# ScalarE's high part of the last unit moves behind its copy of the first product, VectorE's low part one place later

## The chip, the cores and the metric

The kernel runs on one core of a Trainium2 chip. The metric is device time in microseconds (us) of the whole kernel, lower is better. A core has a matrix engine (TensorE; in the profile PE for its matmuls and PEld for its weight loads), three engines for elementwise work (VectorE or DVE, ScalarE or ACT, GpSimd or POOL) and SyncE (SP), which here only issues DMAs. Every engine works through its own queue in program order; between engines there are only semaphores.

## What is computed

Three layers in a row: masked attention, a mixture of eight experts with two chosen per token, and a gated layer on 2304 tokens. Only the gated layer is touched:

```python
rms = np.sqrt(np.mean(x * x, axis=-1, keepdims=True) + 1e-06)
xn = x / rms * rms_g
g = xn @ w_gate
silu = g * (1.0 / (1.0 + np.exp(-g)))
val = xn @ w_val
return (silu * val @ w_out).astype(np.float32)
```

Here x is 2304 x 512, w_gate and w_val are 512 x 1536, w_out is 1536 x 512.

## The kernel before

**Precision.** A number is kept as a high part (rounded to the matmul's format) and a low part (what the rounding left). `mm3` (L149 to L151) makes one product of three matmuls: high by high, high by low, low by high. So wherever a matmul operand is prepared, ScalarE writes the high part and VectorE then subtracts it from the full value to get the low part.

**Tiling.** The gated layer makes three passes of 768 tokens (two groups of 384) over 12 blocks of 128 columns of w_gate and w_val. Four blocks of pass 0 are done plainly; the other 32 (eight of pass 0, twelve each of passes 1 and 2) are *units*. A unit takes both token groups, both halves of the 512 inputs, and gate and value together, as a 2 x 2 by 2 x 2 block product with seven products instead of eight. `product` makes one of them (six matmuls of 384 columns), in the order P1, P6, P7, P5, P4, P2, P3, and `nextb` gives it one of only two PSUM banks, 3 and 6, in turn. A bank comes free when its product has been read: P1 by ScalarE's copy into `p1` (L1294), the others by VectorE's additions. The results are `sgb` (gate times value of the second token group, L1328) and `sga` (of the first, L1338, after P3 at the end of the unit).

**The result's way on.** `to_h` has ScalarE copy the high part of `sga` or `sgb` into a tile `ha` (L1125) and returns the low part's subtraction on VectorE (L1127) for later. `om` multiplies `ha` by w_out: three matmuls of 512 columns. The next unit runs the three `om` of `sgb` after P1, P6 and P7, and the three of `sga` after P5, P4 and P2.

**What else is in a unit.** `whi` and `wlo` split the weights of the next two units in four pieces (L1195 on ScalarE; L1208 on VectorE in pass 0; from pass 1 on the low parts come back by DMA). `comb` runs one of four steps that combine the experts' outputs for the next pass: `weigh` is ScalarE's scaling (L856), then come VectorE's addition (L859) with ScalarE's squares (L860), a root (L863, L864), and a scaling (L874). `tile_T`, in the units with blocks 4 to 9 of passes 0 and 1, transposes a tile of these on TensorE after P1 (L1237), into the *next* of the same two banks, and ScalarE copies it to `xT` (L1239). `extra` splits operands of the next pass, in some units with a copy on ScalarE (L1164) and a subtraction on VectorE (L1166).

**Banks with a transpose.** Without one, P1 takes bank A, P6 bank B, P7 bank A. With one, P1 takes A, the transposes B, P6 A again, P7 B. There P6 needs the copy of P1 (L1294), and P7 the copy to `xT` (L1239). Twelve units are like this.

The order of all queues is written out by hand in `unit`; no scheduler changes it. Around the change it was, at a unit's end and the next one's start: product P3, VectorE's addition and multiplication into `sga`, ScalarE's high part of `sga`, ScalarE's `whi(n + 2, 0)`; then product P1, the copy to `p1`, `comb`, the low part of `sga`, `wlo(n + 1, 0)`, `whi(n + 1, 1)`.

Of the kernel before, what the change touches and what calls it, by code (L numbers as in the profile page):

```python
# [24 lines left out]
def attn_moe_swiglu(ctx: ExitStack, tc: tile.TileContext, q, k, v, w_gate, w_noise, noise, w1, w2,  # L25
# [816 lines left out]
    def fetch(t):  # L842
        YG[t] = []
        for kk in range(2):
            y = buf("yg")
            nc.gpsimd.indirect_dma_start(y, None, yd, bass.IndirectOffsetOnAxis(  # L846
                ap=posu[:, kk, t:t + 1], axis=0))
            YG[t].append(y)

    def combine_parts(t):  # L850
        ya, y2 = YG.pop(t)
        ms = bc.tile([128, 2], F32, name="ms", bufs=2)
        X2[t] = (ya, ms)

        def weigh():
            nc.scalar.activation(ya, ya, AF.Copy, scale=wts[:, t, 0:1])  # L856

        def add():
            nc.vector.scalar_tensor_tensor(ya, y2, wts[:, t, 1:2], ya, op0=OP.mult, op1=OP.add)  # L859
            nc.scalar.activation(y2, ya, AF.Square, accum_out=ms[:, 0:1])  # L860

        def root():
            nc.vector.tensor_scalar(ms[:, 1:2], ms[:, 0:1], 1.0 / DM, 1e-6, op0=OP.mult, op1=OP.add)  # L863
            nc.gpsimd.tensor_tensor(ms[:, 0:1], ms[:, 1:2], mhalf, op=OP.pow)  # L864

        return [weigh, add, root, lambda: norm(t)]
# [246 lines left out]
    sga, sgb, u2, u3, p1 = (gx.tile([128, 384], F32, name=n) for n in ("sga", "sgb", "u2", "u3", "p1"))  # L1113
# [4 lines left out]
    def nextb():  # L1118
        turn["g"] += 1
        return bank[(3, 6)[turn["g"] % 2]][:, :384]  # L1120

    def to_h(p, f, i, sg):

        h = keep.tile([128, 2, 384], F32R, name="ha", bufs=2)
        nc.scalar.copy(h[:, 0], sg)  # L1125
        HG[p, f, i] = h
        return lambda: V.tensor_tensor(h[:, 1], sg, h[:, 0].bitcast(F32), op=OP.subtract)  # L1127

    def om(p, f, i, t):

        h = HG[p, f, i]
        w = slot(cuse["O", f // 2])
        o = (f % 2) * 512
        b = ob[3 * i + t]
        mm3(b, h, w, (slice(t * 128, (t + 1) * 128),), (slice(o, o + 512),), f == 0, f == NFC - 1)
        if f == NFC - 1:
            y = buf("o")
            if t % 2 == 0 or p + 1 < NP:
                nc.scalar.copy(y, b)  # L1139
            else:  # L1140
                V.tensor_copy(y, b)
            r = (p * 6 + i * 3 + t) * 128
            nc.sync.dma_start(out[r:r + 128, :], y)
# [35 lines left out]
    def wload(n):  # L1179
        if n < len(cols):  # L1180
            f = cols[n][1]
            b, c = (wb1, wc1) if n % 2 else [keep.tile([128, 1024], F32, name="stage", bufs=2) for _ in range(2)]
            a = ud[UD.index(("G", f))]
            nc.sync.dma_start(b[:, :512], a[:, :512])
            nc.sync.dma_start(b[:, 512:768], a[:, 768:])
            nc.sync.dma_start(c, uc[f])
            WS[n] = b, c
# [3 lines left out]
    def whi(n, i):  # L1191
        if n < len(cols):
            d = BW[n % 2].rearrange("p s k n -> p s (k n)")
            b, c = WS[n]
            nc.scalar.copy(d[:, 0, slice(*PIECE[i])], (c[:, :512], b[:, :512], c[:, 512:], b[:, 512:768])[i])  # L1195

    def wlo(n, i):

        if n < len(cols):
            p, f = cols[n]  # L1200
            d = BW[n % 2].rearrange("p s k n -> p s (k n)")
            b, c = WS[n]
            sl = slice(*PIECE[i])
            if (p and (p - 1, f) in cols):
                if i == 0:
                    nc.sync.dma_start(d[:, 1].bitcast(F32), ul[f])
            else:
                V.tensor_tensor(d[:, 1, sl], (c[:, :512], b[:, :512], c[:, 512:], b[:, 512:768])[i],  # L1208
                                d[:, 0, sl].bitcast(F32), op=OP.subtract)
                if i == 3:  # L1210
                    nc.sync.dma_start(ul[f], d[:, 1].bitcast(F32))
# [14 lines left out]
    def prod(n, name, b):  # L1226
        a, k = PROD[name]
        for c in range(2):
            o = b, BW[n % 2], SOP[cols[n][0], a], (k, slice(c * 128, (c + 1) * 128)), (c,)
            mm3(*o, c == 0, c == 1)  # L1230

    def tile_T(t):
        ya, _ = X2.pop(t)
        turn["g"] += 1
        b = bank[(3, 6)[turn["g"] % 2]]
        for c in range(4):
            nc.tensor.transpose(b[:, c * 128:(c + 1) * 128], ya[:, c * 128:(c + 1) * 128], identf)  # L1237
        o = (t % 3) * 128
        nc.scalar.copy(xT[t // 3 % 2][:, :, o:o + 128], b.rearrange("p (c n) -> p c n", c=4))  # L1239


    def extras(p, f):
        if p + 1 == NP:
            return []

        def halves(n):
            return [(lambda h=h: split_op(p + 1, n, h, 0), lambda h=h: split_op(p + 1, n, h, 1)) for h in range(2)]

        def part(n, k):
            return None, lambda: sums(n, slice(k * 128, k * 128 + 128))  # L1250

        a11, s2, s3, s1, a22, a12, s4 = (halves(n) for n in ORDER)
        s4s = [(None, lambda k=k: sums("S4", slice(k * 192, k * 192 + 192))) for k in range(2)]
        return {7: [*a11, part("S1", 0), part("S2", 0), part("S3", 0)],
                8: [part(n, 1) for n in ("S1", "S2", "S3")],
                9: [part(n, 2) for n in ("S1", "S2", "S3")] + s2,
                10: s3 + s4s, 11: s1 + a22 + [a12[0]], 12: [a12[1]] + s4}.get(f, [])

    def unit(n):
        p, f = cols[n]  # L1260
        pp_, pf = (p, f - 1) if f else (p - 1, NFC - 1)
        t6 = 6 * (p + 1)
        more = p + 1 < NP
        ex = deque(extras(p, f) if f else extras(p - 1, NFC) if p else [])
        todo = []
        cmb = combine_parts(t6 + f - 3) if more and 3 <= f < 9 else []
        wload(n + 2)

        def om_(i, t):
            if (pp_, pf, i) in HG:  # L1270
                om(pp_, pf, i, t)

        def extra(k=1, last=False):

            while todo:
                todo.pop(0)()
            for _ in range(0 if last else k):
                if ex:
                    hi, lo = ex.popleft()
                    if hi is not None:  # L1280
                        hi()
                    todo.append(lo)

        def comb():
            if cmb:
                cmb.pop(0)()

        def product(name):
            b = nextb()
            prod(n, name, b)  # L1290
            return b

        b = product("P1")
        nc.scalar.copy(p1, b)  # L1294
        comb()
        LO.pop(0)()
        wlo(n + 1, 0)
        whi(n + 1, 1)
        extra()
        om_(1, 0)  # L1300
        if more and 4 <= f < 10:
            tile_T(t6 + f - 4)
        b = product("P6")
        V.tensor_add(u2, b, p1)
        wlo(n + 1, 1)
        whi(n + 1, 2)
        comb()
        extra()
        om_(1, 1)
        b = product("P7")  # L1310
        V.tensor_add(u3, b, u2)
        wlo(n + 1, 2)
        whi(n + 1, 3)
        comb()
        extra()
        om_(1, 2)
        b = product("P5")
        V.tensor_add(sgb, b, u3)
        V.tensor_add(u2, b, u2)
        comb()  # L1320
        extra(2)
        om_(0, 0)
        b = product("P4")
        V.tensor_add(u3, b, u3)  # L1324
        nc.scalar.activation(u3, u3, AF.Silu)  # L1325
        wlo(n + 1, 3)
        extra(last=True)
        V.tensor_mul(sgb, sgb, u3)  # L1328
        lo = to_h(p, f, 1, sgb)
        om_(0, 1)  # L1330
        b = product("P2")
        V.tensor_add(sga, b, p1)
        nc.scalar.activation(sga, sga, AF.Silu)
        lo()
        om_(0, 2)
        b = product("P3")
        V.tensor_add(u2, b, u2)  # L1337
        V.tensor_mul(sga, sga, u2)  # L1338
        LO.append(to_h(p, f, 0, sga))
        whi(n + 2, 0)  # L1340
        if more and 2 <= f < 8:
            fetch(t6 + f - 2)
# [66 lines left out]
            split_op(0, "S4", h, k)  # L1409
    for t in range(3):  # L1410
        om(0, 2, 1, t)
    LO = [lambda: None]
    HG = {k: h for k, h in HG.items() if k == (0, NREG - 1, 1)}
    for n in range(len(cols)):
        unit(n)
    LO.pop()()
    for i in (1, 0):
        for t in range(3):
# [31 lines left out]
```

## Time and profile before

| | |
|---|---|
| time, median of 3 runs | 1095.3 us (1095.11 to 1097.02) |
| the profiled execution, its own time | 1100.19 us |
| its span, first to last instruction | 1098.4 us |
| TensorE matmuls busy | 1051.4 us, 96% |
| TensorE weight loads busy | 944.9 us, 86% |
| VectorE busy | 700.1 us, 64% |
| ScalarE busy | 494.5 us, 45% |

The profile is one execution. Busy times are sums over the whole span; the units begin at about 704 us of it and end at about 1090 us. A row of the timeline has a start, a duration, the engine, the line and the operation, and in brackets how long the engine had stood idle and who released it. Starts of consecutive rows can be nearer than the durations, since instructions overlap in the pipeline, so what an instruction costs its engine is read from start to start.

### The profile page before, as it was taken

What the parts mean: (1) busy time and instruction counts of PE and PEld (TensorE: products, weight loads), DVE (VectorE), ACT (ScalarE), POOL (GpSimd) and SP (SyncE); (2) the same over time, 40 slices, a digit from 0 to 9 for tenths busy, and PEclk for the clock granted to TensorE, in tenths of its full rate; (3) what the DMA queues carried; (4) which work ended last, traced back from release to release, by engine and by line L of the source; (5) the groups of instructions that cost most, each with busy time, mean ns of one, the idle gap of its engine ahead of it and who ended that gap; (6) DMA issues with size and microseconds to landing.
All of it is one profiled execution on the core that took longest, in us unless ns stands there. A gap on an engine that the chain in (4) does not pass through costs nothing. (4 is left out here: it accounts for less than half of the span.)

```text
span 1098.4 us, 17694 instructions
## 1 busy us (share of the span) xinstructions
PE 1051.4 (96%) x6309; PEld 944.9 (86%) x6309; DVE 700.1 (64%) x1489; ACT 494.5 (45%) x1044; POOL 223.1 (20%) x261
## 2 busy tenths in 40 slices
PE   7988989999999999999999999999999999999998
PEld 5776777889989999999898989888999888999997
DVE  4666665457788788876354144878876566754554
ACT  4766652353443444443344144545454554543342
POOL 6565210303232323222200034111000220000000
PEclk8989889999999999999999999999999999999999
DMA  9977522358798898775444133455456554464431
GB/s 162 206 177 162 129 62 64 96 176 267 267 300 279 284 287 296 261 246 184 164 155 143 48 115 98 146 203 174 168 201 231 195 175 148 159 216 166 140 135 58
DMA packets 179418, 196.13 MB, mean 179 GB/s; under 512 B 66816, under 2 KB 135424, under 8 KB 179328
## 3 DMA queue, kind: packets, MB, share of 16 engines
q1 hardware_dynamic: 169264, 172.37, 49.8%
q0 software_dynamic: 9920, 22.35, 7.7%
q8 instruction: 50, 0.82, 0.3%
q14 instruction: 40, 0.33, 0.1%
q10 hardware_dynamic: 144, 0.26, 0.1%
HBM read 140.88 MB, written 54.00 MB: 177 GB/s over the span
## 5 line engine op out<-in xcount | busy, mean ns | idle before, releaser
L149 PE MATMUL bank<-xta,low 128*128 128x384 f32 x376 | 128.0, 340 | 3.1 <-DVE posu L956 2.0
L151 PE MATMUL bank<-xta,low 128*128 128x384 f32 x376 | 127.9, 340 | 0.0
L150 PE MATMUL bank<-xta,low 128*128 128x384 f32 x376 | 127.7, 340 | 0.0
L149 PE MATMUL bank<-ring,ha 128*128 128x512 f32 x288 | 114.3, 397 | 0.0
L150 PE MATMUL bank<-ring,ha 128*128 128x512 f32 x288 | 114.0, 396 | 0.0
L151 PE MATMUL bank<-ring,ha 128*128 128x512 f32 x288 | 114.0, 396 | 0.0
L149 PE MATMUL bank<-low 128*128 128x384 f32 x264 | 89.8, 340 | 7.3 <-ACT p L1294 7.2
L150 PE MATMUL bank<-low 128*128 128x384 f32 x264 | 89.7, 340 | 0.0
L151 PE MATMUL bank<-low 128*128 128x384 f32 x264 | 89.5, 339 | 0.0
L1030 POOL TENSOR_TENSOR dm<-dm,da 128x512 f32<-128x512 f32 x36 | 46.7, 1296 | 203.7 <-DVE da L1028 101.8
L162 ACT ACTIVATE ha<-bank 128x384 fp32r<-128x384 f32 x64 | 31.4, 490 | 116.5 <-PE bank L151 116.4
L149 PEld LDWEIGHTS bank<-xta,low 128*128 128x128 f32 x376 | 71.3, 190 | 11.4 <-issue 3.3
L163 DVE SCALAR_TENSOR_TENSOR ha<-bank,ha 128x384 fp32r<-128x384 f32 x64 | 35.4, 553 | 63.4 <-ACT ha L162 63.3
L150 PEld LDWEIGHTS bank<-xta,low 128*128 128x128 f32 x376 | 71.2, 189 | 4.9
L151 PEld LDWEIGHTS bank<-xta,low 128*128 128x128 f32 x376 | 71.2, 189 | 0.0
L846 POOL DMA_INDIRECT buf<-yd,posu x36 | 38.5, 1069 | 155.2 <-DMA yd<-buf 98.6
L1325 ACT ACTIVATE u<-u 128x384 f32<-128x384 f32 x32 | 16.8, 526 | 115.7 <-DVE u L1324 115.7
L151 PEld LDWEIGHTS bank<-ring,ha 128*128 128x128 f32 x288 | 54.0, 187 | 12.4 <-DVE ha L1127 0.3
L149 PEld LDWEIGHTS bank<-low 128*128 128x128 f32 x264 | 49.6, 188 | 15.7 <-ACT p L1294 9.8
L132 DVE TENSOR_TENSOR low<-stage,low 128x1024 fp32r<-128x1024 f32 x34 | 42.6, 1256 | 23.2 <-ACT low L131 21.4
L830 POOL DMA_INDIRECT buf<-xd,mapu x37 | 47.8, 1291 | 46.7 <-DVE posu L956 16.6
L149 PEld LDWEIGHTS bank<-ring,ha 128*128 128x128 f32 x288 | 54.1, 188 | 3.1 <-ACT ha L1125 0.3
(284 smaller groups left out, 2780.9 us busy)
## 6 DMA issues: line engine op xcount, KB each, us to landing
stage<-in_moe_w_dram SPq DMA_DIRECT2D x128, 256.0 KB
low<-ul SPq DMA_DIRECT2D x20, 896.0 KB
ul<-low SPq DMA_DIRECT2D x12, 896.0 KB
yd<-buf SPq DMA_DIRECT2D x40, 256.0 KB
ud<-dm SPq DMA_DIRECT2D x36, 256.0 KB
stage<-uc SPq DMA_DIRECT2D x16, 512.0 KB
wc<-uc SPq DMA_DIRECT2D x16, 512.0 KB
yd<-zero SPq DMA_DIRECT2D x28, 256.0 KB
```

The lines of the kernel that those rows point to most:

```text
L132: lo_engine.tensor_tensor(r[:, 1], st, r[:, 0].bitcast(F32), op=OP.subtract)
L149: nc.tensor.matmul(o, l[(slice(None), 0) + lsl], r[(slice(None), 0) + rsl], start=first, stop=False)
L150: nc.tensor.matmul(o, l[(slice(None), 0) + lsl], r[(slice(None), 1) + rsl], start=False, stop=False)
L151: nc.tensor.matmul(o, l[(slice(None), 1) + lsl], r[(slice(None), 0) + rsl], start=False, stop=last)
L162: nc.scalar.activation(h[:, 0], p, AF.Relu)
L163: nc.vector.scalar_tensor_tensor(h[:, 1], p, 0.0, h[:, 0].bitcast(F32), op0=OP.max, op1=OP.subtract)
L830: nc.gpsimd.indirect_dma_start(t, None, xd, bass.IndirectOffsetOnAxis(ap=mapu[:, e * NT + j:e * NT + j + 1], axis=0))
L846: nc.gpsimd.indirect_dma_start(y, None, yd, bass.IndirectOffsetOnAxis(ap=posu[:, kk, t:t + 1], axis=0))
L1030: nc.gpsimd.tensor_tensor(m, m, a.bitcast(F32), op=OP.add)
L1325: nc.scalar.activation(u3, u3, AF.Silu)
```

## The change

The high part of `sga` is no longer queued at the end of its own unit. It is kept in a list and queued in the next unit right behind the copy of P1; the low part's subtraction, which was queued before `wlo(n + 1, 0)`, now stands behind VectorE's addition that reads P6. For the first unit and behind the last one the lists are set up so that each part is queued once.

```diff
         b = product("P1")
         nc.scalar.copy(p1, b)
+        HI.pop(0)()
         comb()
-        LO.pop(0)()
         wlo(n + 1, 0)
         whi(n + 1, 1)
         extra()
...
         b = product("P6")
         V.tensor_add(u2, b, p1)
+        for lo in LO[:1]:
+            LO.remove(lo)
+            lo()
         wlo(n + 1, 1)
...
         V.tensor_mul(sga, sga, u2)
-        LO.append(to_h(p, f, 0, sga))
+        HI.append(lambda: LO.append(to_h(p, f, 0, sga)))
         whi(n + 2, 0)
...
-    LO = [lambda: None]
+    HI, LO = [lambda: None], []
...
     for n in range(len(cols)):
         unit(n)
+    HI.pop()()
     LO.pop()()
```

ScalarE's queue, where the second unit of pass 0 (block 5) ends and the third (block 6) begins, before: `sga` is turned into `ha` first, then comes the weight piece (`wc_5918` to `low`), then P1's bank into `p_6865`.

```order
L1333 ACTIVATE sga<-sga 128x384
L1125 CAST ha<-sga 128x384
L1195 CAST low<-wc_5918 128x512
L1294 COPY p_6865<-bank_104 128x384
L856 ACTIVATE buf<-buf,wts 128x512
L1195 CAST low<-wb_6866 128x512
L1239 COPY xT_5916<-bank_107 128x4x128
```

The same place in the changed kernel, whose line numbers from the second product on are 3 higher:

```order
L1336 ACTIVATE sga<-sga 128x384
L1195 CAST low<-wc_5918 128x512
L1294 COPY p_6865<-bank_104 128x384
L1125 CAST ha<-sga 128x384
L856 ACTIVATE buf<-buf,wts 128x512
L1195 CAST low<-wb_6866 128x512
L1239 COPY xT_5916<-bank_107 128x4x128
```

The cast of `sga` went two rows down, past the weight piece and the copy of P1; all the others kept their order.

VectorE's queue at the same place, before: the multiplication into `sga`, its low part, a weight piece, then the addition that reads P6's bank and `p`.

```order
L1338 TENSOR_TENSOR sga<-sga,u_6863 128x384
L1127 TENSOR_TENSOR ha<-sga,ha 128x384
L1208 TENSOR_TENSOR low<-wc_5918,low 128x512
L1304 TENSOR_TENSOR u_6863<-bank_104,p_6865 128x384
L1208 TENSOR_TENSOR low<-wb_6866,low 128x512
L859 SCALAR_TENSOR_TENSOR buf<-buf,wts 128x512
L1311 TENSOR_TENSOR u_6864<-bank_107,u_6863 128x384
```

In the changed kernel:

```order
L1341 TENSOR_TENSOR sga<-sga,u_6863 128x384
L1208 TENSOR_TENSOR low<-wc_5918,low 128x512
L1304 TENSOR_TENSOR u_6863<-bank_104,p_6865 128x384
L1127 TENSOR_TENSOR ha<-sga,ha 128x384
L1208 TENSOR_TENSOR low<-wb_6866,low 128x512
L859 SCALAR_TENSOR_TENSOR buf<-buf,wts 128x512
L1314 TENSOR_TENSOR u_6864<-bank_107,u_6863 128x384
```

The low part went past a weight piece and the addition of P6. On TensorE, SyncE and GpSimd no instruction changed its place.

## Rows read from the trace of the kernel before

**Rows 1.** The page: its head, and TensorE's busy time, share and instructions.

```profile
span 1098.4 us, 17694 instructions
...
PE 1051.4 (96%) x6309; PEld 944.9 (86%) x6309; DVE 700.1 (64%) x1489; ACT 494.5 (45%) x1044; POOL 223.1 (20%) x261
```

**Rows 2.** Busy time by stretch: PE, PEld, DVE, ACT, POOL; granted clock; DMA share; GB/s.

```profile
840.00:930.00 90.00, 86.14 (x448) 78.39 (x448) 54.98 (x109) 42.98 (x93) 15.29 (x16) 1.00 0.55 184
930.00:1090.00 160.00, 160.00 (x829) 148.66 (x828) 89.15 (x164) 64.03 (x135) 0.00 (x0) 1.00 0.43 145
```

**Rows 3.** Waits from 690 us on: total us, times, longest us.

```profile
PEld bank L149 <- ACT p L1294: 9.8, 11, 1.1
PE bank L149 <- ACT p L1294: 7.2, 11, 0.8
...
PEld bank L149 <- ACT xT L1239: 0.9, 2, 0.5
```

**Rows 4.** Timeline of TensorE, third unit of pass 0: P1's end to P6's beginning.

```profile
728.21 0.33 PE L151 MATMUL bank<-xta,low 128*128 128x384 f32 x1
...
729.08 0.60 PE L1237 MATMUL bank<-identf,buf 128*128 128x128 f32 x4
730.31 0.45 PE L149 MATMUL bank<-low 128*128 128x384 f32 x1 [0.64 <-ACT p L1294]
730.60 0.34 PE L150 MATMUL bank<-low 128*128 128x384 f32 x1
...
730.31 0.19 PEld L149 LDWEIGHTS bank<-low 128*128 128x128 f32 x1 [0.87 <-ACT p L1294]
```

**Rows 5.** Timeline of TensorE, first unit: transposes, P6's second matmul, P7's first.

```profile
705.06 0.60 PE L1237 MATMUL bank<-identf,buf 128*128 128x128 f32 x4
...
705.67 0.34 PE L150 MATMUL bank<-low 128*128 128x384 f32 x1
...
707.24 0.33 PE L149 MATMUL bank<-low 128*128 128x384 f32 x1
```

**Rows 6.** Timeline of ScalarE, third unit of pass 0.

```profile
728.85 0.51 ACT L1125 CAST ha<-sga 128x384 fp32r<-128x384 f32 x1 [1.95 <-DVE sga L1338]
729.27 0.61 ACT L1195 CAST low<-wc 128x512 fp32r<-128x512 f32 x1
729.79 0.47 ACT L1294 COPY p<-bank 128x384 f32<-128x384 f32 x1
730.16 0.72 ACT L856 ACTIVATE buf<-buf,wts 128x512 f32<-128x512 f32 x1
...
731.29 0.59 ACT L1239 COPY xT<-bank 128x512 f32<-128x512 f32 x1
```

**Rows 7.** How soon ScalarE follows TensorE: last matmul and copy, pass 1.

```profile
809.36 0.40 PE L151 MATMUL bank<-ring,ha 128*128 128x512 f32 x1
...
809.79 0.59 ACT L1139 COPY buf<-bank 128x512 f32<-128x512 f32 x1 [0.25 <-PE bank L151]
```

**Rows 8.** Timeline of SyncE: the load that the cast at 729.27 reads.

```profile
714.97 1.12 SPq L1186 DMA_DIRECT2D wc<-uc  x1
```

**Rows 9.** Timeline of ScalarE, unit with block 7 of pass 0.

```profile
744.24 0.51 ACT L1164 CAST low<-xT 128x384 fp32r<-128x384 f32 x1
```

**Rows 10.** Timeline of VectorE: third unit of pass 0, then block 7.

```profile
729.40 0.56 DVE L1127 TENSOR_TENSOR ha<-sga,ha 128x384 fp32r<-128x384 f32 x1 [0.64 <-ACT ha L1125]
729.92 0.69 DVE L1208 TENSOR_TENSOR low<-wc,low 128x512 fp32r<-128x512 f32 x1
731.76 0.56 DVE L1304 TENSOR_TENSOR u<-bank,p 128x384 f32<-128x384 f32 x1 [1.15 <-PE bank L151]
...
733.50 0.56 DVE L1311 TENSOR_TENSOR u<-bank,u 128x384 f32<-128x384 f32 x1
...
735.21 0.56 DVE L1318 TENSOR_TENSOR sgb<-bank,u 128x384 f32<-128x384 f32 x1 [0.48 <-PE bank L151]
...
748.48 0.55 DVE L1318 TENSOR_TENSOR sgb<-bank,u 128x384 f32<-128x384 f32 x1
```

## The prediction

> **What bounds the kernel now.** I read the page first: TensorE's matmuls are busy for 96% of a span of 1098.4 us [rows 1], so time can only come out of the places where TensorE stands still. The busy time by stretch says where these are: from 930 us on it is busy in all 160.00 of 160 us, while in the 90 us from 840, where the units carry transposes, it lacks 3.9 us [rows 2]. The granted clock is 1.00 in both stretches, the 2.4 GHz level, so no stretch has a slower clock to win back. The list of waits then names the cause: from 690 us on TensorE waits for ScalarE's copy of P1 (L1294) 11 times, 7.2 us in its matmuls and 9.8 us in its weight loads [rows 3]. The timeline of one such unit shows the pattern. P1's last matmul runs from 728.21 to 728.54, the transposes start at 729.08, and then P6, which needs P1's bank back, stands until 730.31 [rows 4]. ScalarE explains the lateness: the copy starts only at 729.79, 1.25 us after P1 was ready, because the high part of `sga` (728.85, released by VectorE's multiplication) and a weight piece (729.27) stand ahead of it [rows 6]. The eleven are the units with a transpose but the first one; the first has no last unit's high part ahead of its copy and does not wait. In the other twenty units P6 has another bank, and the copy's lateness is covered by P6 itself.
>
> **What a removed stall is worth.** The idle time of 0.64 us in P6's row understates it, since the first matmul after it is also longer (0.45 us) [rows 4]. I compare with the first unit, where nothing waits: from the start of the transposes to P6's second matmul it takes 705.67 - 705.06 = 0.61 us [rows 5], in the stalled unit 730.60 - 729.08 = 1.52 us [rows 4]. The stall costs 0.91 us. Ten are alike, and one is the longest of the list, 1.1 us [rows 3]: 10 x 0.91 + 1.1 = 10.2 us in all. This is the most that the change can give back, since the trace shows in these units only two further waits, on `xT` [rows 3], beside short ones in the first unit that nothing of the change touches.
> The Trainium skill, "Perfetto Trace Analysis", section Identifying the Most-Contended Engine, says that matmul busy time misleads because pipelined matmuls look smaller, and that weight-load time is the better measure. By its measure the sum would be 9.8 us and by matmul idle time 7.2 us; the trace, with 0.91 us from start to start, sides with the weight loads.
>
> **The high part moved (ScalarE).** Nothing is added or removed, one cast of 0.42 us from start to start (728.85 to 729.27) moves behind the copy [rows 6]. What does the copy wait for then? The weight piece still ahead of it needs its load, which was issued at 714.97 [rows 8], 13.6 us before P1 ends; and it can run while ScalarE stood idle 1.95 us before the high part [rows 6]. So I take it as done, and the copy starts with P1's end. ScalarE follows TensorE by 809.79 - (809.36 + 0.40) = 0.03 us [rows 7], which gives 728.57, and an end at 729.04. P6 on the unstalled course would start its second matmul at 729.08 + 0.61 = 729.69; the copy is out of the way by over half a microsecond, and the stall should go as a whole.
>
> **What is late next: the copy to `xT`.** P7 needs its bank. In the new order ScalarE's row of starts is copy 728.57, high part 0.37 later (728.94; its multiplication was done by 728.85), `weigh` 0.42 later (729.36), then `weigh` and a weight piece 731.29 - 730.16 = 1.13 us (730.49), and 0.59 us for the copy itself: 731.08 [rows 6]. A release takes about 0.05 us (copy end 729.79 + 0.47 = 730.26, P6 at 730.31 [rows 4, 6]), so P7 could start at 731.13. Unstalled it starts 707.24 - 705.06 = 2.18 us after the transposes [rows 5], here at 731.26. So 0.13 us is left, of which a late release would take 0.1 for the longer first matmul: nearly nothing, and this is the tightest place. I take zero loss; the bound on the other side is the 0.42 us of the moved cast.
> Three kinds of unit differ. In the two with block 7 a further cast of the same size as the moved one (0.51 us at 744.24 [rows 9], so 0.42 us from start to start) stands ahead of the copy to `xT`; these are the two waits of 0.9 us in all [rows 3]. There the copy to `xT` comes earlier by the 1.22 us that the copy of P1 gains (729.79 to 728.57) less 0.42 us, so 0.8 us, while P6 comes 0.91 us earlier: the wait grows by 0.1 us, 0.2 us for both. In the first stalled unit TensorE's P1 is nearer to the multiplication and the high part may hold the queue: 0.1 us. In the two with block 9 there is no `weigh`, and the margin is wide.
>
> **The low part moved (VectorE).** It no longer waits 0.64 us for ScalarE ahead of a weight piece, but costs about 0.5 us (729.40 to 729.92) behind P6's addition [rows 10]. The addition of P7 behind it starts later after its product by that much; in this unit VectorE had 0.48 us of idle time ahead of P5's addition (735.21), and that takes it up [rows 10]. P7's bank is wanted again by P4, behind P5, so a P7 addition that is 0.5 us later still ends before P5's addition and nobody waits: cost 0. Without that cover it would be 0.5 us a unit. The low part itself and the high part are read by `om` only behind P5, two products later. The units without a transpose and the end of the kernel keep their time: TensorE is busy without a gap there, and the last high part has the same neighbours as before.
>
> **Sum.** 10.2 - 0.2 - 0.1 = 9.9 us; I take 9.8, as seven units have only that margin of 0.03 us behind a late release. The profiled execution is at 1100.19 us with a span of 1098.4 us, 0.3 to 0.4% above the median of 1095.3; scaled, 9.8 us stays 9.8. **Forecast 1085.5 us**, its own range 1084.4 to 1086.8: all of 10.2 us and a quicker run below, 0.2 us more lost in each of seven units above.
>
> **Rivals.**
> *Weight loads hidden in the wait.* If P6's first weights were loaded while the copy runs, only the idle time of the matmuls is lost now, and 7.2 us come back: 1088.1 us. Against it: P6's weight load starts at 730.31, with its matmul and not ahead of it [rows 4]. Chance 0.07. The Trainium skill's "TensorE: Matmul & The Clock Gate", section Architectural detail, says that TensorE may pull weight loads ahead of matmuls in flight, which would speak for this; the trace does not show it at this wait.
> *The stall moves to `xT`.* If the moved cast costs ScalarE more than its 0.42 us, or the multiplication into `sga` comes later than P1's copy, P7 waits instead. At 0.25 us in each of the nine units with `weigh` this takes 2.2 us: 1087.7 us; the bound of 0.42 us each gives 1089.3. For it: the margin of 0.03 us. Chance 0.12.
> *The copy stays late.* The change does nothing if the weight piece still ahead of the copy is held until about 729.3 by its load or by the matmuls that read the buffer before. That needs a load of more than 14 us; with such loads TensorE would be seen to wait for DMAs, and it does not [rows 3, 8]. 1095.3 us. Chance 0.05.
> *Slower: the low part on the path.* If VectorE has no idle time left behind P6's addition, 0.5 us of low part delays each later addition and at last a bank. In the unit with block 7 of pass 0 P5's addition has indeed no idle time ahead of it (748.48 [rows 10]). It decides where the delay passes one product and its `om`, about 1.7 us (731.76 to 733.50). In all 31 units it would cost 15.5 us, less 9.8: 1101.0 us. Against it: VectorE is busy 55.0 of 90 us in the stretch of pass 1 [rows 2]. Chance 0.03.
>
> **How the numbers follow.** The forecast has 0.73. The range 1084.4 to 1088.6 takes in the first rival and most of the second, and leaves out the last two and the tails, under 0.2. 0.2% is 2.2 us, about what a measurement of this kernel tells from no change: faster 0.73 + 0.07 + 0.12 = 0.92, same 0.05, slower 0.03.
>
> **What the profile after would show.** Right: no waits of TensorE for L1294; the copy starting within 0.1 us of P1's end, the high part behind it; the transposes' units 0.9 us shorter; TensorE idle 7 us less from 700 us on; waits for `xT` in two units, slightly longer than 0.5 us. Wrong: waits for L1239 in nine units, for a VectorE addition in P4 or P2, or for `ha` in `om`. The forecast fails if ScalarE's starts lie further apart in the new order than in the old.

## The result, and the profile after

The changed kernel takes 1086.92 us (median of five runs, 1086.51 to 1088.64), the kernel before in the runs beside it 1096.04 us: ratio 0.9908, 95% interval 0.9891 to 0.9925, so 9.1 us less. In later runs, where the kernel before took 1099.37 us, the changed kernel took 1089.41 us: ratio 0.9910 (0.9896 to 0.9924).

The page of the changed kernel (head and busy times) and its busy time by stretch (as [rows 2]):

```profile
span 1086.9 us, 17666 instructions
...
PE 1045.1 (96%) x6309; PEld 941.3 (87%) x6309; DVE 697.8 (64%) x1489; ACT 494.4 (45%) x1044; POOL 220.5 (20%) x261
```

```profile
840.00:930.00 90.00, 89.83 (x477) 82.80 (x476) 57.88 (x114) 45.78 (x99) 11.96 (x14) 1.00 0.52 179
930.00:1080.00 150.00, 150.00 (x775) 139.04 (x774) 81.13 (x152) 58.76 (x125) 0.00 (x0) 1.00 0.41 142
```

In the stretch from 840 us TensorE lacked 3.9 us before [rows 2]; now it lacks 0.2. The clock is the same, 1.00. The span fell by 11.5 us, more than the median, and not all of that is the change's: ahead of the first multiplication into `sga`, where no instruction stands in another place, this one execution was 1.8 us shorter (713.51 against 715.27 below; more on this at the end). What the change moves is best read inside the trace, from the first multiplication into `sga` to the last (32 units, timeline of VectorE). Before:

```profile
715.27 0.56 DVE L1338 TENSOR_TENSOR sga<-sga,u 128x384 f32<-128x384 f32 x1
728.21 0.56 DVE L1338 TENSOR_TENSOR sga<-sga,u 128x384 f32<-128x384 f32 x1
741.15 0.56 DVE L1338 TENSOR_TENSOR sga<-sga,u 128x384 f32<-128x384 f32 x1
754.37 0.56 DVE L1338 TENSOR_TENSOR sga<-sga,u 128x384 f32<-128x384 f32 x1
767.32 0.56 DVE L1338 TENSOR_TENSOR sga<-sga,u 128x384 f32<-128x384 f32 x1
...
1090.14 0.56 DVE L1338 TENSOR_TENSOR sga<-sga,u 128x384 f32<-128x384 f32 x1
```

The timeline of the changed kernel: these multiplications; then the third unit of pass 0 on TensorE, ScalarE and VectorE, and of the first unit, which has no high part ahead of it, two matmuls of TensorE:

```profile
713.51 0.56 DVE L1341 TENSOR_TENSOR sga<-sga,u 128x384 f32<-128x384 f32 x1
725.34 0.56 DVE L1341 TENSOR_TENSOR sga<-sga,u 128x384 f32<-128x384 f32 x1
737.39 0.56 DVE L1341 TENSOR_TENSOR sga<-sga,u 128x384 f32<-128x384 f32 x1
750.01 0.56 DVE L1341 TENSOR_TENSOR sga<-sga,u 128x384 f32<-128x384 f32 x1
761.89 0.56 DVE L1341 TENSOR_TENSOR sga<-sga,u 128x384 f32<-128x384 f32 x1
...
1078.61 0.56 DVE L1341 TENSOR_TENSOR sga<-sga,u 128x384 f32<-128x384 f32 x1
...
725.35 0.33 PE L151 MATMUL bank<-xta,low 128*128 128x384 f32 x1
...
726.21 0.60 PE L1237 MATMUL bank<-identf,buf 128*128 128x128 f32 x4
726.57 0.42 PE L149 MATMUL bank<-low 128*128 128x384 f32 x1
726.83 0.34 PE L150 MATMUL bank<-low 128*128 128x384 f32 x1
...
728.62 0.34 PE L150 MATMUL bank<-low 128*128 128x384 f32 x1
...
723.94 0.60 ACT L1195 CAST low<-wc 128x512 fp32r<-128x512 f32 x1
725.77 0.48 ACT L1294 COPY p<-bank 128x384 f32<-128x384 f32 x1 [1.23 <-PE bank L151]
726.15 0.52 ACT L1125 CAST ha<-sga 128x384 fp32r<-128x384 f32 x1
726.56 0.72 ACT L856 ACTIVATE buf<-buf,wts 128x512 f32<-128x512 f32 x1
...
727.70 0.59 ACT L1239 COPY xT<-bank 128x512 f32<-128x512 f32 x1
...
728.45 0.55 DVE L1127 TENSOR_TENSOR ha<-sga,ha 128x384 fp32r<-128x384 f32 x1
...
731.45 0.56 DVE L1321 TENSOR_TENSOR sgb<-bank,u 128x384 f32<-128x384 f32 x1
...
703.91 0.34 PE L150 MATMUL bank<-low 128*128 128x384 f32 x1
...
705.65 0.34 PE L150 MATMUL bank<-low 128*128 128x384 f32 x1
```

The 31 steps between the multiplications took 1090.14 - 715.27 = 374.87 us before and 1078.61 - 713.51 = 365.10 us now: 9.77 us less. The step from 728.21 to 741.15 was 12.94 us, that from 725.34 to 737.39 is 12.05. P6's second matmul now follows the transposes by 726.83 - 726.21 = 0.62 us, where it was 1.52 [rows 4] and 0.61 in the unit that never waited [rows 5]. And the reader sees why in ScalarE's rows: the weight piece runs at 723.94, the queue then stands 1.23 us for P1 itself, and the copy starts 0.09 us after P1's end (725.35 + 0.33 = 725.68), where it was 1.25 us. The waits from 690 us on, as [rows 3]:

```profile
PE bank L149 <- ACT xT L1239: 0.3, 2, 0.2
...
PEld bank L149 <- ACT xT L1239: 2.6, 9, 0.6
```

L1294 has left the list. The copy to `xT` stands in it nine times, where it stood twice.

### The profile page after: what moved, and what is told of

The parts are those of the page before. It is cut to its first block, busy times and chain, and to the rows that moved or that the text cites. A ratio compares the mean times of both kernels' runs of the same rounds, so it can differ in the third digit from the quotient of the medians.

```text
span 1086.9 us, 17666 instructions
## 1 busy us (share of the span) xinstructions
PE 1045.1 (96%) x6309; PEld 941.3 (87%) x6309; DVE 697.8 (64%) x1489; ACT 494.4 (45%) x1044; POOL 220.5 (20%) x261
## 5 line engine op out<-in xcount | busy, mean ns | idle before, releaser
L162 ACT ACTIVATE ha<-bank 128x384 fp32r<-128x384 f32 x64 | 31.3, 489 | 110.8 <-PE bank L151 110.7
L151 PEld LDWEIGHTS bank<-ring,ha 128*128 128x128 f32 x288 | 54.0, 187 | 12.4 <-DVE ha L1127 0.3
L131 ACT CAST low<-stage 128x1024 fp32r<-128x1024 f32 x42 | 44.2, 1053 | 30.0 <-DMA stage<-in_moe_w_dram 29.7
L149 PEld LDWEIGHTS bank<-ring,ha 128*128 128x128 f32 x288 | 54.1, 188 | 3.1 <-ACT ha L1125 0.3
L150 PEld LDWEIGHTS bank<-ring,ha 128*128 128x128 f32 x288 | 54.1, 188 | 2.8
```

The costliest lines, as they stand in the source:

```text
L131: nc.scalar.copy(r[:, 0], st)
L149: nc.tensor.matmul(o, l[(slice(None), 0) + lsl], r[(slice(None), 0) + rsl], start=first, stop=False)
L150: nc.tensor.matmul(o, l[(slice(None), 0) + lsl], r[(slice(None), 1) + rsl], start=False, stop=False)
L151: nc.tensor.matmul(o, l[(slice(None), 1) + lsl], r[(slice(None), 0) + rsl], start=False, stop=last)
L162: nc.scalar.activation(h[:, 0], p, AF.Relu)
```

## The experiments

Outside the units the traces of these kernels differ by up to 3.6 us with the same instructions (span less the 31 steps: 721.1 to 724.7 us; e6 alone has one more cast at its end), so each run is read twice: by its ratio to the kernel before, run beside it, and by the 31 steps inside its trace. The kernel before took 1099.4 us beside the experiments and 1096.04 us in the first runs, so the whole times that the expectations name are to be read as differences from it or from the changed kernel.

| run | ratio to before (95% interval) | 31 steps, us |
|---|---|---|
| before | | 374.87 |
| the change | 0.9908 (0.9891 to 0.9925) | 365.10 |
| a0, the change again | 0.9910 (0.9896 to 0.9924) | 365.17 |
| e1, high part alone | 0.9905 (0.9889 to 0.9920) | 365.18 |
| e2, low part alone | 1.0012 (1.0002 to 1.0023) | 375.01 |
| e3, weight piece away | 0.9955 (0.9940 to 0.9970) | 370.62 |
| e4, high part behind `xT` | 0.9895 (0.9878 to 0.9912) | 364.58 |
| e5, low part twice | 0.9935 (0.9921 to 0.9949) | 366.09 |
| e6, high part twice | 0.9964 (0.9951 to 0.9977) | 369.71 |
| e7, split behind `xT` | 0.9920 (0.9905 to 0.9935) | 364.46 |

**The change again.** The same kernel, as the measure for the runs beside it.

> The changed kernel once more, as the measure for the runs beside it. The stretch of the units, from the first multiplication into sga to the last, comes out at 365.1 us as in its first profile (374.9 us before), and the ratio to before inside 0.989 to 0.993.

Timeline of VectorE, first and last multiplication into `sga`:

```profile
715.42 0.56 DVE L1341 TENSOR_TENSOR sga<-sga,u 128x384 f32<-128x384 f32 x1
...
1080.59 0.56 DVE L1341 TENSOR_TENSOR sga<-sga,u 128x384 f32<-128x384 f32 x1
```

365.17 us: the steps repeat to 0.1 us, while this execution's span, 1088.8 us, is 1.9 us longer than the first one's. Two executions of one kernel are few, but the steps of single units agree as well, to 0.01 us in most. So the 31 steps tell tenths, and the times do not.

**The two halves of the change.** First the high part alone, the low part back where it was:

```diff
         nc.scalar.copy(p1, b)
         HI.pop(0)()
         comb()
+        for lo in LO[:1]:
+            LO.remove(lo)
+            lo()
         wlo(n + 1, 0)
...
         V.tensor_add(u2, b, p1)
-        for lo in LO[:1]:
-            LO.remove(lo)
-            lo()
         wlo(n + 1, 1)
```

> The high part of sga stands behind the copy of P1 as in the change, the low part is back in its old place ahead of weight piece 0. Theory (all of the gain is that ScalarE frees P1's bank earlier): TensorE has no wait for L1294 in the eleven units, and the time is that of the changed kernel, about 1087 us, within 0.7 us. Rival (the low part's new place gives VectorE time that TensorE then gets): at least 2 us slower than the changed kernel, with TensorE or its weight loads waiting for VectorE additions.

Then the low part alone, made from the kernel before:

```diff
         nc.scalar.copy(p1, b)
         comb()
-        LO.pop(0)()
         wlo(n + 1, 0)
...
         V.tensor_add(u2, b, p1)
+        LO.pop(0)()
         wlo(n + 1, 1)
```

> Only the low part moves behind P6's addition, the high part stays at the end of its unit. Theory: eleven waits for L1294 stay as they are, 7.2 us in matmuls and 9.8 us in weight loads, and the time is that of before, 1096 us within 0.7 us. Rival (low part on the path): 0.5 us lost in each unit in which VectorE has no idle time, 1100 us or more.

The waits of e1:

```profile
PEld bank L149 <- ACT xT L1239: 2.6, 9, 0.6
```

and of e2:

```profile
PE bank L149 <- ACT p L1294: 7.5, 11, 0.9
...
PEld bank L149 <- ACT p L1294: 10.1, 11, 1.1
```

With the high part alone L1294 is gone from the list and the steps take 365.18 us, as in the whole change; with the low part alone the eleven waits are all there and the steps take 375.01 us. The gain is the high part's; the low part's new place neither helps nor costs, but for 0.3 us that e2 loses at block 7 of pass 0 (13.50 us instead of 13.22) and in part gets back elsewhere. e2's ratio lies a little above 1, by 1.3 us, more than the 0.7 us of the expectation and more than the 0.14 us of its steps. The rest lies outside the units; its runs had a lower mean granted clock than those of the kernel before beside it (median 0.983 against 0.985), and such runs are longer, as the last section shows.

**The other instruction ahead of the copy.** The high part and the low part stay as before; the weight piece between the high part and the copy goes behind P6's addition.

```diff
         nc.scalar.copy(p1, b)
         comb()
         LO.pop(0)()
-        wlo(n + 1, 0)
         whi(n + 1, 1)
...
         V.tensor_add(u2, b, p1)
+        if n:
+            whi(n + 1, 0)
+        wlo(n + 1, 0)
         wlo(n + 1, 1)
...
-        whi(n + 2, 0)
```

> The high part and the low part stay where they were; the weight piece 0 that stood between the high part and the copy of P1 goes behind P6's addition instead (its low part with it). Theory (the stall is the sum of what the copy has ahead of it): the copy starts 0.52 us earlier (the step from 729.27 to 729.79), so each of the eleven stalls shrinks from 0.91 to 0.39 us and 5.7 us are gained: 1090.3 us. Rival (only idle time of matmuls counts, weight loads hide the rest): 11 x 0.52 of 0.64 us leaves 0.12 us a unit, but less than 4 us gained in time. Rival (the stall moves to the copy to xT): gain under 3 us with nine waits for L1239.

The timeline of e3 (ScalarE; of VectorE the multiplications into `sga` and a low part of weights in the unit with block 7 of pass 0), and its waits:

```profile
729.31 0.51 ACT L1125 CAST ha<-sga 128x384 fp32r<-128x384 f32 x1 [1.96 <-DVE sga L1340]
729.73 0.47 ACT L1294 COPY p<-bank 128x384 f32<-128x384 f32 x1
...
728.67 0.56 DVE L1340 TENSOR_TENSOR sga<-sga,u 128x384 f32<-128x384 f32 x1
741.07 0.56 DVE L1340 TENSOR_TENSOR sga<-sga,u 128x384 f32<-128x384 f32 x1
754.84 0.56 DVE L1340 TENSOR_TENSOR sga<-sga,u 128x384 f32<-128x384 f32 x1
...
745.19 1.29 DVE L1208 TENSOR_TENSOR low<-stage,low 128x512 fp32r<-128x512 f32 x2 [0.52 <-ACT low L1195]
```

```profile
PEld bank L149 <- ACT p L1294: 4.7, 11, 0.6
...
PEld bank L149 <- DVE sga L1334: 1.4, 3, 0.7
```

The ordinary unit does what the theory says: the copy follows the high part by 0.42 us instead of 0.94, and the step is 741.07 - 728.67 = 12.40 us, 0.54 shorter. The steps sum to only 4.25 us less, not 5.7, and both rivals with the smaller gains stay wrong for the ordinary unit. Most of what is missing was lost at block 7 of pass 0 (754.84 - 741.07 = 13.77 us, before 13.22) and in the unit behind it (12.78 us instead of 12.40). At block 7 the late weight piece left VectorE idle for 0.52 us (745.19), and P1 of the next two units then waited for an addition (L1334: three waits in the list, of which one, for the first unit's addition, stands in every run).

**What ends next.** If it is the copy to `xT`, a second cast of the high part behind the copy of P1 must cost time in the units with `weigh` and nowhere else:

```diff
         nc.scalar.copy(h[:, 0], sg)
+        if i == 0 and (p or f >= NREG):
+            nc.scalar.copy(h[:, 0], sg)
         HG[p, f, i] = h
```

> The changed kernel with the cast of the high part of sga queued twice in a row behind the copy of P1 (the second writes the same values). Theory (the copy to xT is what ends next, and nothing is left of its margin): 0.42 us in each of the nine units with weigh and 0.4 us at the kernel's end, about 4 us slower than the changed kernel, with the waits for L1239 at 0.6 us in seven units and at 1.0 us in two. In the two units with block 9 and the twenty without transposes nothing. Rival (the waits for L1239 do not lengthen the units): 0.4 us at the end alone.

Its waits, with L1241 for the copy to `xT` and L1127 for the second cast; then the end of P1 and ScalarE's rows in the third unit of pass 0:

```profile
PE bank L149 <- ACT xT L1241: 3.1, 9, 0.7
PE bank L149 <- ACT ha L1127: 0.4, 1, 0.4
...
PEld bank L149 <- ACT xT L1241: 7.0, 9, 1.1
```

```profile
728.10 0.33 PE L151 MATMUL bank<-xta,low 128*128 128x384 f32 x1
...
728.47 0.48 ACT L1296 COPY p<-bank 128x384 f32<-128x384 f32 x1 [1.17 <-PE bank L151]
728.85 0.52 ACT L1125 CAST ha<-sga 128x384 fp32r<-128x384 f32 x1
729.39 0.51 ACT L1127 CAST ha<-sga 128x384 fp32r<-128x384 f32 x1
729.81 0.72 ACT L856 ACTIVATE buf<-buf,wts 128x512 f32<-128x512 f32 x1
```

The steps take 4.5 us more than those of a0, 0.50 us in an ordinary one of the nine units, and not a tenth in the two with block 9 or the twenty without transposes; the 0.4 us at the end is the row of L1127. By the ratio it is 5.9 us, against the 4 us expected. The margin is used up, as expected. That an ordinary unit loses 0.50 us and not 0.42 stands in the rows: the two casts start 0.54 us apart, where an instruction behind a cast starts 0.41 us after it in the change (726.15 to 726.56), so from the copy to `weigh` it takes 1.34 us instead of 0.79, which is 0.55 more, less the 0.05 us by which the copy starts sooner after P1's end (0.04 us, where it was 0.09). Why two casts of the same tile lie further apart is not shown.

And the other way, the high part behind the copy to `xT`, with the low part behind one more weight piece:

```diff
         nc.scalar.copy(p1, b)
-        HI.pop(0)()
         comb()
...
             tile_T(t6 + f - 4)
+        HI.pop(0)()
         b = product("P6")
         V.tensor_add(u2, b, p1)
+        wlo(n + 1, 1)
         for lo in LO[:1]:
             LO.remove(lo)
             lo()
-        wlo(n + 1, 1)
```

> As the changed kernel, but the high part stands behind the copy to xT (behind the place of the transposes in units without one), and the low part one further place later, behind weight piece 1. Theory (what is left is the copy to xT, 0.42 us late for the cast): the waits for L1239 go, in the two units with block 7 they cost 0.59 and 0.44 us now, in the others under 0.05 us each: about 1 us faster than the changed kernel, 1086.0 us. Rival (those waits cost nothing, or the later high part makes VectorE wait and P7's addition late): the same time or slower, 1087 us or more.

Its waits:

```profile
PEld bank L149 <- DVE sga L1335: 1.0, 2, 0.6
PEld bank L149 <- ACT xT L1239: 0.4, 2, 0.2
```

The steps are 0.5 us shorter than the change's, not 1. Pass 1's unit with block 7 went from 12.47 to 12.06 us as expected; pass 0's stayed at 12.62 and the one behind it went from 11.88 to 11.77, 0.1 us for the two, because there P1 of the next unit now waits for VectorE's addition (L1335, twice and 1.0 us, where it was once and 0.6, for the first unit's addition). In the other units with `weigh` the waits for L1239 are gone, and their steps, but for the one behind block 7, are the same to 0.01 us: those waits had cost next to nothing. The last experiment moves the other late instruction instead, the splitting cast, and puts the low part back where it was before the change, as in e1:

```diff
         whi(n + 1, 1)
-        extra()
         om_(1, 0)
         if more and 4 <= f < 10:
             tile_T(t6 + f - 4)
+        extra()
```

> The high part behind the copy of P1, the low part back in its old place, and the splitting step of the next pass (one cast on ScalarE, one subtraction on VectorE) behind the copy to xT instead of ahead of it. Theory (the stalls that are left are that cast in the two units with block 7): both units at about 12.05 us instead of 12.45, so 0.8 us faster than the changed kernel, and no wait for L1239 over 0.2 us. Rival (in pass 0 VectorE's backlog ends there, as with the high part behind xT, and P1 waits for an addition instead): only pass 1's unit gets shorter, 0.4 us.

Its multiplications into `sga` (timeline of VectorE), on both sides of block 7 of pass 0, and its waits:

```profile
740.18 0.56 DVE L1341 TENSOR_TENSOR sga<-sga,u 128x384 f32<-128x384 f32 x1
752.26 0.56 DVE L1341 TENSOR_TENSOR sga<-sga,u 128x384 f32<-128x384 f32 x1
```

```profile
PEld bank L149 <- ACT xT L1239: 1.8, 9, 0.2
```

Both units with block 7 take 12.06 to 12.08 us and no wait for `xT` is over 0.2 us; the steps are 0.7 us shorter than those of a0. The times cannot tell this: e7's ratio and the change's have overlapping intervals, and so has e4's. So there is a version with shorter units than both kernels, and none shown to be faster than the change.

**VectorE's cover.** The low part's subtraction twice in a row:

```diff
             LO.remove(lo)
             lo()
+            lo()
```

> The changed kernel with the subtraction of the low part queued twice in a row (the second writes the same values). Theory (the low part behind P6's addition lies in VectorE's idle time): under 1 us slower than the changed kernel, what there is in the unit with block 7 of pass 0. Rival (low part on the path): 0.47 us in each of the 31 units, 15 us slower, or 4 us if it is so in the eight units of pass 0 alone.

Its multiplications into `sga` (timeline of VectorE), on both sides of block 7 of pass 0:

```profile
739.69 0.56 DVE L1342 TENSOR_TENSOR sga<-sga,u 128x384 f32<-128x384 f32 x1
753.25 0.56 DVE L1342 TENSOR_TENSOR sga<-sga,u 128x384 f32<-128x384 f32 x1 [0.46 <-DVE u L1341]
```

The steps are 0.9 us longer than those of a0, and all of it is in this one unit, 13.56 us instead of 12.62. Thirty units carry another half microsecond of VectorE without notice. The ratio says 2.7 us, with an interval that just meets the change's; what lies beyond the 0.9 us is not in the units. These runs too had a lower mean granted clock (median 0.983 against 0.985 for a0).

## Why the prediction was right

**What bounds, and what a stall is worth.** The eleven waits of TensorE for the copy of P1 were the gain. 0.91 us a stall held: the ordinary step fell by 0.89 us (12.94 to 12.05). The idle time of the matmuls, 0.64 us, would have given 7.2 us, so the rival in which weight loads hide in the wait is out. The Trainium skill's "Perfetto Trace Analysis", section Identifying the Most-Contended Engine, says that TensorE's matmul busy time is a poor measure of how near it is to its peak, and names weight-load busy time as one of two better ones; it speaks of busy shares, not of the price of a stall. This case's trace points the same way: the weight loads had waited 9.8 us for L1294, the matmuls 7.2, and the steps fell by 9.77. That 9.8 and 9.77 are so near is partly luck, since the stalls come to 10.2 us from start to start and 0.4 us of it did not come back.

**The high part moved.** The copy starts 0.09 us after P1 where 0.03 was taken, and the stall is gone as a whole. That it was the queue ahead of the copy is shown from two sides: the high part alone gives all of it, the weight piece alone 0.54 us in an ordinary unit, about its own 0.52. From the first to the last unit TensorE's idle time fell by the 7 us forecast (7.7 us from 704 to 1090 us before, 0.7 us from 702.2 to 1078.5 us now). The rival that the copy stays late is out: the weight piece now runs 1.8 us ahead of the copy.

**What is late next.** The copy to `xT` was named, and the zero margin was right to within the 0.06 us by which the copy of P1 starts later than taken. From P6's second matmul to P7's second it takes 728.62 - 726.83 = 1.79 us, where the first unit has 705.65 - 703.91 = 1.74: at most 0.05 us lost, beside seven new waits of 0.2 us in the weight loads. The whole step shows 0.01: 12.05 us, where the units with block 9, which have no such wait, take 12.04. The prediction named waits for L1239 in nine units as a sign that it was wrong, and waits in two as right; nine came, and it was right in time all the same, because the sign was not tied to a length. The two with block 7 kept a longer wait, 0.6 where it was 0.5, as worked out. e6 shows that the rival's mechanism was real and only its size was not: 0.55 us more of queue, and 4.5 us of the 9.8 are gone. That a margin of hundredths held was partly luck: the readings that it was added up from are themselves good to some hundredths.

**The low part moved.** Free, as taken; it lies in VectorE's idle time, which e2 and e5 show, but for the unit with block 7 of pass 0. In the third unit the 0.48 us that VectorE had stood idle ahead of P5's addition are gone from its row (731.45), as worked out. At block 7 VectorE has no idle time left: the step into it fell by only 0.60 us and the next by 1.07 (13.22 and 12.95 to 12.62 and 11.88), together 1.67. With the low part in its old place (e1) they fell by 0.77 and 0.90, also 1.67, so there only VectorE's multiplication came later, and TensorE lost nothing. The slower rival had the right place and not the cost: the change itself loses nothing there, and a second low part (e5) loses 0.9 us there and nothing in the other thirty.

**The sum.** 9.8 us were forecast for the units and 9.77 came, nearer than its terms deserve, since they missed both ways. The ordinary stall gave 0.89 us and not 0.91, 0.2 us less over ten; the first stalled unit gave its whole 1.11 us (12.94 to 11.83), so the 0.1 us set against it was too much; block 7 took back about 0.25 us in its two units, where 0.2 was set. The forecast of 1085.5 us is 1.4 us under the median, of which 0.7 is the kernel before, which was at 1096.04 and not 1095.3 in these runs; the rest is within the interval of the ratio. One reading was loose without harm: the copy's margin of over half a microsecond was taken to P6's second matmul, and P6's first starts some 0.25 us earlier (726.57 in the changed kernel, where the copy ends at 725.77 + 0.48 = 726.25).

## What to carry to other kernels

On an in-order engine, look at what stands ahead of the instruction that frees a buffer, and move anything whose reader comes much later behind it; price the stall from start to start against a place that has none, not by the idle column. Then walk the same queue on to the next release: what stands behind the moved instruction comes later by its whole length, and here the next release had next to nothing to spare: half a microsecond more of queue took back nearly half the gain. Where the units repeat, compare them inside the trace, since tenths of a microsecond show there that whole runs do not tell.

## What was not expected

What lies outside the 31 steps (span less steps), nearly all of it ahead of the units and with the same instructions in all kernels, took from 721.1 to 724.7 us in the ten profiled executions, while the steps of one kernel repeated to 0.1 us. Against this scatter a change of 0.2% is not to be had from a few whole times. The traces say where it arises: ScalarE's first activation of the experts (L162) starts between 173.7 and 177.7 us, so the scatter is all there before 180 us. It goes with TensorE's granted clock. From 100 to 200 us this was 0.93 in the two executions with the least time outside the steps (the changed kernel's and e2's) and 0.90 or 0.91 in the other eight, and it was 1.00, the 2.4 GHz level, in the units. Whole runs say the same: of the 17 of the kernel before beside e1 to e4, the three at a mean clock of 0.981 took 1101.15 to 1103.62 us, the nine at 0.985 took 1097.67 to 1100.50. No run sets the clock, so that it is the cause is not shown.

And a wait of 0.2 us in the list of weight loads cost about 0.01 us by the steps, 0.05 at most: the list shows the time since the last weight load, not what the matmuls lose, and nine waits instead of two, read alone, would have misled.
